# Attention and feed-forward on one core: GpSimd's additions made to wait for VectorE, another order of two half-array matmuls, and a new plan

## The chip, the core and the metric

The kernel runs on one core of a Trainium2 chip. The metric is the device time of one execution in microseconds, median of the runs. The core's engines each work through a queue of their own, in order: PE (TensorE, matmuls; its weight loads are shown as PEld), DVE (VectorE), ACT (ScalarE), POOL (GpSimd), and SP, which here only issues transfers.

## The reference, cut to what matters

```python
# q, k, v: (4, 8, 1152, 64)
q_pool = q.reshape(B, H, S // 2, 2, D).mean(axis=3)
scores = scale * np.matmul(q_pool, k.transpose(0, 1, 3, 2))
attn = np.exp(scores - np.max(scores, axis=-1, keepdims=True))
attn = attn / (np.sum(attn, axis=-1, keepdims=True) + 1e-09)
x = np.matmul(attn, v)          # then the heads side by side: (4 * 576, 8 * 64) = (2304, 512)
h = x @ w_in                     # 512 -> 2048
g = np.maximum(h, 0.0) + alpha * np.minimum(h, 0.0)
out = g @ w_out                  # 2048 -> 512
```

There are 32 heads with 576 pooled queries and 1152 keys each, and a feed-forward of 2304 tokens.

## The kernel before

Two heads are worked on together, as a pair, since a head has only 64 features: head 0 of the pair lies in rows 0 to 63 of the array of PE and head 1 in rows 64 to 127, and a matmul of 64 rows leaves the other half of the array to its neighbour. A pair's 576 queries are cut into two halves of 288, so there are 32 "half-heads", one after the other; in each of them nine blocks of 128 keys pass through four steps.

- **Scores** (line 951): eight matmuls a block, for x in four products, for i in the two heads. Numbers are split into a high and a low part so that float32 is kept: k1 and q1 are the high parts, k2 (line 699) and q2 (line 691) the low ones, and the fourth product subtracts the maxima. `ps` is a pair of PSUM banks, one for each head.
- **Exponentials** (line 968) on ACT, one for each head, from PSUM into the tile `pa`.
- **Sums of the exponentials** over the key blocks (line 981): of the seven additions of a half-head, the blocks 6 and 8 (`ADDS`) are added on DVE and five on POOL. At the end of a pair PE adds up the partitions (line 1017).
- **Weighted values** (line 995): 18 matmuls in a row at the end of the half-head, each of which the trace shows as two.

Between the score blocks stand the **maxima blocks** of the next pair: one matmul of 384 keys (line 818, one head each, heads taken in turn) or two of 288 (line 825, both on the same head), whose maximum DVE takes out of PSUM (line 839, into `bx`). 24 of the first kind and 8 matmuls of the second belong to a pair. The result of a pair is divided by its sums on DVE (line 1054, `r`), and split (line 1061 on ACT, line 1066 on DVE), and stored; all these DVE operations, like the low parts q2 and k2 and the conversion of the weights (lines 391 to 427), read two tensors from SBUF.

The feed-forward (line 479) runs partly between the last half-heads, and alone from about 445 us on, with 128-row matmuls.

The order of all instructions is made in Python before the kernel is built, by the class `Scheduler`. `add` records a task with an engine, a planned duration, what it reads and writes and a priority; `run` picks again and again the task that can start first by the planned times, with the smallest priority value among those within a slack, and `place` emits it. Tasks with `lock=True` (the DVE operations with two SBUF inputs and POOL's additions) are planned one after the other over both engines: `place` sets `lock_free` to the end of such a task and no other of them is planned before that. In the kernel before, that holds in the plan alone; on the chip each engine follows its own queue and waits only for its data. The numbers in the signature of `attention_ffn` are planned costs, slacks and priorities, and which PSUM banks scores, maxima and feed-forward may take early (`EARLY`) and after half-head 13 (`LATE`).

Of the kernel before, what the change touches and what calls it, by code (L numbers as in the profile page):

```python
# [108 lines left out]
class Scheduler:  # L109
# [3 lines left out]
    def __init__(self, col_cost, turn, to_pe, from_pe, slack, dma_fixed):  # L113
        self.tasks, self.ready = [], [[] for _ in range(5)]
        self.free = [0.0] * 5
        self.dma_free = 0.0
        self.now = 0.0
        self.col = 0
        self.lock_free = 0.0
        self.turn = turn  # L120
        self.col_cost, self.to_pe, self.from_pe, self.slack = col_cost, to_pe, from_pe, slack
        self.dma_fixed = dma_fixed
        self.hold = ()

    def add(self, eng, dur, emit, reads=(), writes=(), uses=(), deps=(), prio=0.0, col=0, size=0, kind=None, dma=False, lock=False, fixed=None):
        t = Task()
# [70 lines left out]
    def place(self, at, t):  # L197
        for b in t.takes:
            if b.t is None:
                b.ring.take(b)  # L200
        self.now = at
        t.emit()
        self.ready[t.eng].remove(t)
        dur = t.dur
        if t.eng == PE:
            if t.col != self.col:
                dur += ENTER if t.col else LEAVE
            self.col = t.col
        if t.lock:
            self.lock_free = at + dur  # L210
        self.free[t.eng] = at + dur
        t.end = at + dur
        if t.dma:
            self.dma_free = max(self.dma_free, t.end + 650) + t.size / DMA_RATE
            t.end = self.dma_free
            t.avail = t.end + (self.dma_fixed if t.fixed is None else t.fixed)
        else:
            t.avail = t.end + SYNC
        for n in t.next:
            n.left -= 1  # L220
            if not n.left:
                self.ready[n.eng].append(n)
# [3 lines left out]
def attention_ffn(  # L226
# [8 lines left out]
    NLO: int = 5,  # L235
    PB: int = 13,
    QB: int = 2,
    DF: int = 1985,
    D0: int = 1153.836,
    AQ: int = 0,  # L240
    F0: float = 7.572,
    F2: float = 0.839,
    FD: tuple = (1, 1, 1),
    WE: float = 24.0,
    WG: int = 1,
    WT: float = 6.74,
    WM: int = 2,
    WB: int = 300,
    WN: int = 2,
    TO_PE: int = 89,  # L250
    FROM_PE: int = 40,
    SLP: int = 45,
    SLA: int = 48,
    SLD: int = 138,
    QL: float = -0.025,
    KL: float = 1.207,
    KR: float = 1.497,
    KS: float = 0.082,
    M0: float = 1.211,
    E0: float = 1.868,  # L260
    BD: int = 7,
    SD: tuple = (3, 20),
    LD: tuple = (0, 33),
    TD: tuple = (3, 33),
    SR: float = 0.311,
    KQ: float = 0.342,
    KKB: int = 2,
    FQ: int = 1,
    FB: tuple = (1, 7),
    SF: int = -39,  # L270
    Q0: float = -2.2,
# [5 lines left out]
    ADDS: tuple = ((4, 6, 8), (6, 8)),  # L277
    PL: int = 0,
    LV: int = -2,
    LW: int = -8,  # L280
    GSB: int = 1,
    YSB: int = 4,
    R0: float = 4.187,
    R1: float = -5.36,
    R2: float = -7.727,
    R3: float = -0.231,
    W0: float = 5.34,
    W1: float = 1.69,
    W2: float = 18.088,
    W3: float = 0.137,  # L290
    YL: float = 0.337,
    MS: float = 0.136,
    EARLY: tuple = ((1, 2, 3, 4, 6), (0, 5, 6), ()),
    LATE: tuple = ((0, 1, 2, 3, 4, 5, 6), (0, 1, 2, 3, 4, 5, 6), (1, 2, 3, 4, 5, 6)),
    SWITCH: int = 13,
    GL: float = 23.364,
    COL: float = 0.151,
    HW: float = -1.194,
    XB: int = 4,
    PT: int = 17,  # L300
    VB: int = 4,
# [4 lines left out]
    QA: float = 1.0,  # L306
    REUSE: int = 6,
    NW: tuple = (464, 460, 460, 460, 460),
    RP: float = 31.088,
    RS: float = -1.017,  # L310
    RM: int = 30,
    RATE: float = 342.662,
):
    nc = tc.nc
# [33 lines left out]
    DMA_RATE = RATE  # L348
    sch = Scheduler(COL, SF, TO_PE, FROM_PE, (SLP, SLA, SLD, 0, 0), DF)
    add = sch.add  # L350

    def dt(name, shape, dtype):
        return dram.tile(shape, dtype, tag=name, name=name)
# [29 lines left out]
    def w_split(f, i, mag, prio, ring, left):  # L383
        w = Buf(ring)

        def high():
            w_tiles(f, i, w)
            nc.scalar.activation(out=wh[f, i], in_=mag.t, func=AF.Copy)

        def low():  # L390
            nc.vector.tensor_tensor(
                out=wl[f, i], in0=mag.t, in1=wh[f, i].bitcast(F32), op=ALU.subtract
            )

        t = add(ACT, act(DMO), high, reads=[mag], writes=[w], deps=left, prio=prio)
        add(DVE, dve(DMO), low, reads=[mag], writes=[w], deps=[t], prio=prio, lock=True)
        w_done[f, i] = w

    def w_convert(f, i, prio, release=(), ring=None, left=(), first=()):
# [6 lines left out]
            nc.scalar.activation(out=mag.t, in_=raw.t[:, :, 1].bitcast(F32), func=AF.Abs)  # L406

        def top():
            nc.vector.tensor_scalar(
                out=bits.t, in0=raw.t[:, :, 1], scalar1=3, scalar2=0x3FFFFFF8,  # L410
                op0=ALU.logical_shift_left, op1=ALU.bitwise_and,
            )

        def tail():
            nc.vector.scalar_tensor_tensor(  # L415
                out=bits.t, in0=raw.t[:, :, 0], scalar=29, in1=bits.t,
                op0=ALU.logical_shift_right, op1=ALU.bitwise_or,
            )

        def sign():  # L420
            nc.vector.scalar_tensor_tensor(
                out=bits.t, in0=raw.t[:, :, 1], scalar=-0x40000000, in1=bits.t,
                op0=ALU.bitwise_and, op1=ALU.bitwise_or,
            )

        def value():
            nc.vector.scalar_tensor_tensor(
                out=mag.t, in0=mag.t, scalar=F64_TINY, in1=bits.t.bitcast(F32),
                op0=ALU.is_ge, op1=ALU.mult,
            )  # L430
# [361 lines left out]
    def pair_max(n, w):  # L792
# [15 lines left out]
        for x, (t, j, i) in enumerate(items):  # L808
# [125 lines left out]
    def half_main(n, h, w):  # L934
# [7 lines left out]
        for c in range(NC):  # L942
# [1 line left out]
            p, ps = Buf(r_p), Buf(r_ps)  # L944
            at = n + h + c / NC

            def scores(ps=ps, s=s):
# [286 lines left out]
```

## Time and profile before

| | |
|---|---|
| time before, median of 3 runs | 842.04 us (840.05 to 842.55) |
| the profiled execution's own time | 839.95 us |
| its span | 838.2 us |
| busy PE / DVE / ACT / POOL | 825.2 / 567.0 / 437.4 / 262.4 us |

The span runs from the first to the last profiled instruction; 1.75 us of the execution's time lie around it. PE is nearly always busy in the sense that some matmul is in flight, but two matmuls of 64 rows can be in flight at once, so this share says nothing on how well the halves of the array are filled. The stages are the start (to about 20 us), attention with weight conversion (20 to 200), attention alone (200 to 390), attention mixed with the feed-forward (390 to 445), and the feed-forward.

### The profile page before, as it was taken

To read this page: it belongs to the slowest core of one execution; us is meant where nothing else is said; L and a number is where in the kernel's file an instruction comes from. 1 tells how busy PE (TensorE), PEld (TensorE's weight loads), DVE (VectorE), ACT (ScalarE), POOL (GpSimd) and SP (SyncE) were. 2 spreads that over 40 slices of the span, in tenths; PEclk is the share of its full clock that TensorE was granted. 3 is DMA by queue.
4 is the path that set the end of the run, shared out by engine and by line. 5 is a ranking of instruction groups with operands and counts; after the bars stand their busy time and mean duration, and the time that the engine had idled before them with its cause. 6 is when DMAs were issued, how large, how long until landed. Compare 5 with 4: busy or idle time off the path is not lost.

```text
span 838.2 us, 17447 instructions
## 1 busy us (share of the span) xinstructions
PE 825.2 (98%) x6690; PEld 691.4 (82%) x6690; DVE 567.0 (68%) x1035; ACT 437.4 (52%) x1124; POOL 262.4 (31%) x196
## 2 busy tenths in 40 slices
PE   8999999999999999999999999999999999999997
PEld 8767777676777777776779999998898988988986
DVE  7999999999998988889963799632242232322422
ACT  4657676675766676665754676643232233332321
POOL 5665665565565665654550000000000000000000
PEclk9999999999999999999999999999999999999999
DMA  8234345634354433323233768581330421300301
GB/s 274 58 89 164 82 144 140 197 115 123 87 179 122 122 116 77 83 72 109 69 124 121 248 195 260 177 228 58 91 92 3 120 59 46 91 0 1 91 1 45
DMA packets 67759, 93.71 MB, mean 112 GB/s; under 512 B 20004, under 2 KB 45404, under 8 KB 67676
## 3 DMA queue, kind: packets, MB, share of 16 engines
q1 hardware_dynamic: 65516, 88.18, 33.9%
q0 software_dynamic: 2160, 4.42, 3.6%
q8 instruction: 52, 0.85, 0.4%
q14 instruction: 31, 0.25, 0.1%
HBM read 73.48 MB, written 19.02 MB: 110 GB/s over the span
## 4 chain that ended last, share of the span: by engine, by line
PE 86%; DVE 9%; DMA 2%; issue 1%; ACT 1%; SPq 0%; DVEq 0%; ACTq 0%
PE bank L479 44%; PE bank L951 18%; PE bank L995 15%; PE bank L818 6%; DVE bx L839 3%; PE bank L1017 2%; DMA wraw<-wt 1%; DVE x L1066 1%; DVE pa L981 1%; PE bank L825 1%; PE bank L1129 1%; DMA kk<-kt 1%; DVE pos L515 1%; DVE r L1054 0%; DVE wbits L415 0%
## 5 line engine op out<-in xcount | busy, mean ns | idle before, releaser
L981 POOL TENSOR_TENSOR pa<-pa,pa 128x576 f32<-128x576 f32 x160 | 240.5, 1520 | 155.9 <-ACT pa L968 104.4
L839 DVE TENSOR_REDUCE bx<-bank 128x1 f32<-128x384 f32 (+1 forms) x448 | 214.0, 533 | 22.5 <-PE bank L818 19.9
L968 ACT ACTIVATE pa<-bank 128x288 f32<-128x288 f32 x576 | 199.7, 417 | 25.9 <-PE bank L951 17.4
L951 PE MATMUL bank<-q,k 64*128 64x288 f32 x1728 | 206.2, 311 | 0.8 <-DVE mq L923 0.6
L951 PEld LDWEIGHTS bank<-q,k 64*128 64x128 f32 x1728 | 163.3, 184 | 21.1 <-issue 9.3
L995 PE MATMUL bank<-pa,vv 128*64 128x288 f32 x1152 | 146.8, 409 | 0.0
L995 PEld LDWEIGHTS bank<-pa,vv 128*64 128x64 f32 x1152 | 79.9, 137 | 54.8 <-issue 3.8
L526 DVE TENSOR_TENSOR gw<-gs,gw 128x460 fp32r<-128x460 f32 (+1 forms) x55 | 35.1, 638 | 121.2 <-ACT gw L521 121.2
L951 PE MATMUL bank<-mq,neg 64*128 64x288 f32 x576 | 115.2, 291 | 0.0
L818 PE MATMUL bank<-k,q 64*128 64x384 f32 x384 | 110.1, 362 | 3.5 <-DVE bx L839 2.0
L521 ACT ACTIVATE gw<-gs 128x460 fp32r<-128x460 f32 (+1 forms) x55 | 32.4, 589 | 126.7 <-PE bank L479 115.2
L479 PE MATMUL bank<-wlow,wh 128*128 128x460 f32 (+1 forms) x320 | 93.0, 371 | 0.0
L479 PE MATMUL bank<-gw,wh 128*128 128x460 f32 (+1 forms) x320 | 92.8, 371 | 0.0
L951 PEld LDWEIGHTS bank<-mq,neg 64*128 64x128 f32 x576 | 83.3, 184 | 0.0
L818 PEld LDWEIGHTS bank<-k,q 64*128 64x128 f32 x384 | 62.4, 185 | 16.2 <-DVE bx L839 10.0
L515 DVE SCALAR_TENSOR_TENSOR gs<-gs,nal 128x460 f32<-128x460 f32 (+1 forms) x55 | 38.4, 699 | 52.9 <-ACT gs L510 52.9
L479 PE MATMUL bank<-x,wlow 128*128 128x288 f32 x480 | 66.3, 296 | 0.0
L479 PEld LDWEIGHTS bank<-wlow,wh 128*128 128x128 f32 x320 | 60.0, 188 | 7.1
L479 PE MATMUL bank<-gs,wlow 128*128 128x288 f32 x480 | 65.8, 295 | 0.1
L479 PEld LDWEIGHTS bank<-gw,wh 128*128 128x128 f32 x320 | 60.1, 188 | 6.8
L479 PEld LDWEIGHTS bank<-x,wlow 128*128 128x128 f32 x480 | 64.2, 188 | 1.6 <-issue 1.4
L479 PEld LDWEIGHTS bank<-gs,wlow 128*128 128x128 f32 x480 | 63.9, 188 | 1.4 <-DVE gs L526 0.5
(90 smaller groups left out, 1006.2 us busy)
## 6 DMA issues: line engine op xcount, KB each, us to landing
wraw<-wt SPq DMA_DIRECT2D x32, 512.0 KB
vv<-vt SPq DMA_DIRECT2D x32, 288.0 KB
xs<-x SPq DMA_DIRECT2D x32, 288.0 KB
x<-xs SPq DMA_DIRECT2D x32, 288.0 KB
kk<-kt SPq DMA_DIRECT2D x15, 576.0 KB
r<-rrd SPq DMA_DIRECT2D x64, 72.0 KB
yp<-ys SPq DMA_DIRECT2D x32, 144.0 KB
wlow<-xs SPq DMA_DIRECT2D x16, 288.0 KB
```

The costliest lines, as they stand in the source:

```text
L479: nc.tensor.matmul(out=ps[:, :n], lhsT=w[a, c // DMO][:, c % DMO:c % DMO + P], rhs=lo(hl), start=(first and i == 0), stop=(last and i == 2),)
L515: lambda: nc.vector.scalar_tensor_tensor(out=flat(pos), in0=flat(neg), scalar=nal[:, f:f + 1], in1=flat(pos), op0=ALU.mult, op1=ALU.add),
L521: ACT, act(n), lambda: nc.scalar.activation(out=gs.t[:, 0, :n], in_=flat(pos), func=AF.Copy),
L526: lambda: nc.vector.tensor_tensor(out=gs.t[:, 1, :n], in0=flat(pos), in1=gs.t[:, 0, :n].bitcast(F32), op=ALU.subtract),
L818: nc.tensor.matmul(out=ms.t[:, :JW], lhsT=w.q1.t[d, starts[t]:starts[t] + P], rhs=w.k1.t[d, j * JW:(j + 1) * JW], start=True, stop=True,)
L825: nc.tensor.matmul(out=ms.t[:, :S // 4], lhsT=w.rt.t[d, D - D * u:D - D * u + P], rhs=w.k1.t[d, c:c + S // 4], start=u == 0, stop=u == 1,)
L839: nc.vector.tensor_reduce(out=bx.t[:, at, j:j + 1], in_=ms.t[:, :m], axis=AX.X, op=ALU.max)
L951: nc.tensor.matmul(out=ps.t[i][:, :HQ], lhsT=k.t[d, s] if k else neg[d], rhs=r.t[d, q], start=x == 0, stop=x == len(pairs) - 1,)
L968: lambda ps=ps, p=p, i=i: nc.scalar.activation(out=p.t[:, i], in_=ps.t[i][:, :HQ], func=AF.Exp, scale=SCALE),
L981: lambda a=a, b=p, part=part, e=e: e.tensor_tensor(out=part.t, in0=a.t, in1=b.t, op=ALU.add),
L995: nc.tensor.matmul(out=av.t[i * D:(i + 1) * D, :HQ], lhsT=w.vv[i].t[:, e], rhs=p.t[:, i], start=(e == 0), stop=(e == NC - 1),)
L1017: nc.tensor.matmul(out=ps.t[g * 32:(g + 1) * 32, :HQ], lhsT=ones, rhs=acc[n + g // 2][j].t[:, g % 2], start=j == 0, stop=j == m - 1, tile_ ...
```

## The change

Three things change. First, `place` now keeps the last emitted DVE instruction with `lock=True` as `port`, and gives every emitted POOL instruction with `lock=True` a dependence on it, so that POOL waits on DVE's semaphore. (The conversions return their instruction now, so that it can be kept.) Second, a score block starts with the head whose half of the array the matmul planned before it did not use (`sch.tile`), and the exponentials follow that order. Third, the planned durations of maxima blocks are 108 and 165 instead of 130 and 190, and the numbers of the plan are set anew, so that the whole order is another one.

```diff
         self.hold = ()
+        self.port, self.after = None, None
+        self.tile = 1
...
         self.now = at
-        t.emit()
+        made = t.emit()
+        if t.lock and made is not None:
+            if t.eng == DVE:
+                self.port = made
+            elif self.port is not None:
+                self.after(made, self.port)
...
-    DF: int = 1985,
+    DF: int = 2010,
-    WT: float = 6.74,
+    WT: float = 5.439,
-    KR: float = 1.497,
+    KR: float = 2.229,
-    EARLY: tuple = ((1, 2, 3, 4, 6), (0, 5, 6), ()),
+    EARLY: tuple = ((1, 2, 3, 4, 5), (0, 5, 6), ()),
-    LATE: tuple = ((0, 1, 2, 3, 4, 5, 6), (0, 1, 2, 3, 4, 5, 6), (1, 2, 3, 4, 5, 6)),
+    LATE: tuple = ((0, 1, 2, 3, 4, 5, 6), (0, 5, 6), (3, 4, 5, 6)),
...
+    sch.after = lambda late, early: tc.add_manual_dep(
+        late.ins, early.ins.name, mybir.DependencyInfo(mybir.DependencyClass.Sync, mybir.DependencyReason.DATA),
+        reason="order on the shared port",
+    )
...
-            def rows(t=t, j=j, d=d, ms=ms):
+            def rows(t=t, j=j, d=d, ms=ms, i=i):
+                sch.tile = i
...
-            dur = 190 if rest else 130
+            dur = 165 if rest else 108
...
+            order = []
+
+            def scores(ps=ps, s=s, order=order):
                 pairs = ((w.k1, w.q1), (w.k1, w.q2), (w.k2, w.q1), (None, w.mq))
+                order.extend((1, 0) if sch.tile == 0 else (0, 1))
+                sch.tile = order[1]
                 for x, (k, r) in enumerate(pairs):
-                    for i, d in enumerate(both):
+                    for i in order:
+                        d = both[i]
...
-                    lambda ps=ps, p=p, i=i: nc.scalar.activation(
-                        out=p.t[:, i], in_=ps.t[i][:, :HQ], func=AF.Exp, scale=SCALE
+                    lambda ps=ps, p=p, o=order, i=i: nc.scalar.activation(
+                        out=p.t[:, o[i]], in_=ps.t[o[i]][:, :HQ], func=AF.Exp, scale=SCALE
                     ),
```

What the new order looks like in the instruction queues is shown at three places. All are in the stage of attention alone (DVE's and POOL's near 280 us of the trace before); line numbers of the changed kernel are 11 to 17 higher.

DVE's queue, at the end of a half-head, before: `r` and `x` are the results of the pair (lines 1054 and 1066), `q` and `k` the low parts of a later pair (lines 691 and 699), `bx` the maxima.

```order
L1054 TENSOR_TENSOR r<-avs,r 128x288 x2
L981 TENSOR_TENSOR pa_102<-pa_102,pa_91 128x576
L839 TENSOR_REDUCE bx_114<-bank_122 128x1
L839 TENSOR_REDUCE bx_114<-bank_119 128x1
L839 TENSOR_REDUCE bx_114<-bank_121 128x1
L1066 TENSOR_TENSOR x_4110<-r,x_4110 128x288
L1066 TENSOR_TENSOR x_4114<-r,x_4114 128x288
L981 TENSOR_TENSOR pa_102<-pa_102,pa_93 128x576
L691 TENSOR_TENSOR q_4125<-qs,q_3710 128x576
L699 TENSOR_TENSOR k_4135<-kk,k_3756 128x1152
```

The same place in the changed kernel (lines 1071, 1083, 702, 710):

```order
L1071 TENSOR_TENSOR r<-avs,r 128x288
L998 TENSOR_TENSOR pa_101<-pa_101,pa_91 128x576
L1071 TENSOR_TENSOR r<-avs,r 128x288
L1083 TENSOR_TENSOR x_4115<-r,x_4115 128x288
L851 TENSOR_REDUCE bx_114<-bank_118 128x1
L851 TENSOR_REDUCE bx_114<-bank_124 128x1
L851 TENSOR_REDUCE bx_114<-bank_123 128x1
L1083 TENSOR_TENSOR x_4141<-r,x_4141 128x288
L998 TENSOR_TENSOR pa_101<-pa_101,pa_93 128x576
L702 TENSOR_TENSOR q_4155<-qs,q_3761 128x576
L710 TENSOR_TENSOR k_4157<-kk,k_3837 128x1152
```

The two results are no longer side by side: one DVE addition now stands between the two `r`, and one split goes ahead of the three maxima instead of both behind them. The additions and the low parts follow as before.

POOL's queue at the same place, before: `pa` are the exponentials and their sums, `qs` the second half of a later pair's queries, which POOL loads.

```order
L981 TENSOR_TENSOR pa_102<-pa_89,pa_90 128x576 [waits Activation_49]
L981 TENSOR_TENSOR pa_102<-pa_102,pa_92 128x576 [waits DVE_49,Activation_49]
L981 TENSOR_TENSOR pa_103<-pa_94,pa_97 128x576 [waits Activation_49]
L981 TENSOR_TENSOR pa_103<-pa_103,pa_100 128x576 [waits Activation_49,Pool_49]
L981 TENSOR_TENSOR pa_103<-pa_103,pa_88 128x576 [waits Activation_49,Pool_49]
L981 TENSOR_TENSOR pa_96<-pa_89,pa_90 128x576 [waits Activation_49]
L656 DMA qs<-qt 128x576 [waits DMAHW4_49,DMASW2_49,DVE_49]
L981 TENSOR_TENSOR pa_96<-pa_96,pa_92 128x576 [waits DVE_49,Activation_49]
```

In the changed kernel:

```order
L998 TENSOR_TENSOR pa_101<-pa_89,pa_90 128x576 [waits Activation_49]
L998 TENSOR_TENSOR pa_101<-pa_101,pa_92 128x576 [waits DVE_49]
L998 TENSOR_TENSOR pa_103<-pa_94,pa_97 128x576 [waits DVE_49,Activation_49]
L998 TENSOR_TENSOR pa_103<-pa_103,pa_99 128x576 [waits Activation_49,Pool_49]
L667 DMA qs<-qt 128x576 [waits DMAHW2_49,DMASW2_49]
L998 TENSOR_TENSOR pa_103<-pa_103,pa_88 128x576 [waits Activation_49,Pool_49]
L998 TENSOR_TENSOR pa_96<-pa_89,pa_90 128x576 [waits Activation_49]
L998 TENSOR_TENSOR pa_95<-pa_98,pa_100 128x576 [waits DVE_49,PE_49,Activation_49]
```

The third row, the first addition of a new half-head, now waits for DVE too, by its position in the plan for the low part `k` that ends the DVE rows above; the load of `qs` moves up by two additions. Of the 160 additions of line 981, 33 wait for DVE before the change and 71 after it.

PE's queue at a single maxima block of head 0 between two score blocks, before: the first two rows end a score block (head 0, head 1), and the bank with the lower number is always that of head 0.

```order
L951 MATMUL bank_119<-mq_111,neg 128x288
L951 MATMUL bank_122<-mq_111,neg 128x288
L818 MATMUL bank_120<-k_3359,q_3340 128x384
L951 MATMUL bank_123<-q_2602,k_2645 128x288
L951 MATMUL bank_124<-q_2602,k_2645 128x288
L951 MATMUL bank_123<-q_3040,k_2645 128x288
L951 MATMUL bank_124<-q_3040,k_2645 128x288
```

In the changed kernel, again with a single maxima block of head 0 (line 830) between two score blocks (line 968):

```order
L968 MATMUL bank_121<-mq_112,neg 128x288
L968 MATMUL bank_122<-mq_112,neg 128x288
L830 MATMUL bank_123<-k_3392,q_3345 128x384
L968 MATMUL bank_120<-q_2978,k_3025 128x288
L968 MATMUL bank_119<-q_2978,k_3025 128x288
L968 MATMUL bank_120<-q_3587,k_3025 128x288
L968 MATMUL bank_119<-q_3587,k_3025 128x288
```

After the maxima block of head 0 the score block now starts with the higher bank, that of head 1. Counted over the whole queue, neighbours on the same half among the score and maxima matmuls fall by 210, from 297 to 87 with the fillers and the two-matmul maxima blocks counted; changes between matmul shapes (64 rows, 128 rows, 64 or 32 columns) rise from 98 to 103, and the filler matmuls of the start (line 1129) from 136 to 150. The feed-forward's matmuls are as many as before.

## Rows read from the trace of the kernel before

**Rows 1.** The page's line of busy time, share and instructions.
```profile
PE 825.2 (98%) x6690; PEld 691.4 (82%) x6690; DVE 567.0 (68%) x1035; ACT 437.4 (52%) x1124; POOL 262.4 (31%) x196
```

**Rows 2.** Stages: length, busy PE, PEld, DVE, ACT, POOL (instructions), clock, DMA share, GB/s.
```profile
20.00:200.00 180.00, 177.60 (x1844) 133.86 (x1844) 173.65 (x337) 120.25 (x337) 113.27 (x77) 1.00 0.44 125
200.00:390.00 190.00, 187.67 (x1979) 140.57 (x1978) 169.52 (x320) 123.15 (x345) 112.74 (x81) 1.00 0.36 106
390.00:445.00 55.00, 55.00 (x525) 42.86 (x524) 43.70 (x59) 34.06 (x97) 25.48 (x16) 1.00 0.33 104
```

**Rows 3.** Shares by engine of the chain that ended last.
```profile
PE 86%; DVE 9%; DMA 2%; issue 1%; ACT 1%; SPq 0%; DVEq 0%; ACTq 0%
```

**Rows 4.** Waits, whole span: who waited for whom, us in total, times, longest.
```profile
POOL pa L981 <- ACT pa L968: 104.4, 38, 6.1
...
ACT rt L680 <- DMA qs<-qt: 15.7, 6, 3.9
...
PEld bank L818 <- DVE bx L839: 10.0, 36, 1.0
PEld bank L951 <- issue: 9.3, 22, 0.5
```

**Rows 5.** Lines 1066 and 981: duration ns min/median/max, first and last start.
```profile
L1066 DVE TENSOR_TENSOR x<-r,x x32: 443/656/1673, 72.1 to 461.5; 128x288 fp32r<-128x288 f32 x32
L981 POOL TENSOR_TENSOR pa<-pa,pa x160: 1389/1427/4784, 21.4 to 434.4; 128x576 f32<-128x576 f32 x160
...
L981 DVE TENSOR_TENSOR pa<-pa,pa x64: 684/748/1975, 29.6 to 440.1; 128x576 f32<-128x576 f32 x64
```

**Rows 6.** Timeline of DVE and POOL, 278 to 289 us: start, length, instruction.
```profile
280.14 2.24 DVE L1066 TENSOR_TENSOR x<-r,x 128x288 fp32r<-128x288 f32 x2
...
283.64 1.34 DVE L699 TENSOR_TENSOR k<-kk,k 128x1152 fp32r<-128x1152 f32 x1
...
279.07 2.99 POOL L981 TENSOR_TENSOR pa<-pa,pa 128x576 f32<-128x576 f32 x2 [1.87 <-ACT k L684]
285.41 4.32 POOL L981 TENSOR_TENSOR pa<-pa,pa 128x576 f32<-128x576 f32 x3 [3.35 <-ACT pa L968]
```

**Rows 7.** Timeline of DVE: the first and the last overtaken operations of the stages.
```profile
51.18 1.56 DVE L981 TENSOR_TENSOR pa<-pa,pa 128x576 f32<-128x576 f32 x1
...
174.94 1.67 DVE L1066 TENSOR_TENSOR x<-r,x 128x288 fp32r<-128x288 f32 x1
...
202.47 2.24 DVE L1066 TENSOR_TENSOR x<-r,x 128x288 fp32r<-128x288 f32 x2
...
382.20 1.96 DVE L981 TENSOR_TENSOR pa<-pa,pa 128x576 f32<-128x576 f32 x1
...
434.76 1.66 DVE L1054 TENSOR_TENSOR r<-avs,r 128x288 f32<-128x288 f32 x1
```

**Rows 8.** Line 818 on PE by stage, first 20 to 200, then 200 to 390.
```profile
L818 PEld LDWEIGHTS bank<-k,q 64*128 64x128 f32 x185 | 29.7, 184 | 10.3 <-DVE bx L839 6.8 <-ACT rs L1029 1.4 <-issue 0.5
...
L818 PEld LDWEIGHTS bank<-k,q 64*128 64x128 f32 x177 | 28.8, 184 | 4.4 <-DVE bx L839 2.9 <-issue 0.9
```

**Rows 9.** Timeline of PE: pairs of maxima blocks between scores, 287 and 360 us.
```profile
287.54 0.72 PE L951 MATMUL bank<-q,k 64*128 64x288 f32 x6
...
288.30 0.76 PE L951 MATMUL bank<-q,k 64*128 64x288 f32 x6
...
360.43 0.36 PE L951 MATMUL bank<-q,k 64*128 64x288 f32 x1
...
361.37 0.62 PE L951 MATMUL bank<-q,k 64*128 64x288 f32 x5
```

**Rows 10.** Timeline of ACT and PE about 340 us: a load of queries awaited.
```profile
344.46 0.26 ACT L680 ACTIVATE rt<-qs 128x64 fp32r<-128x64 f32 x1 [3.94 <-DMA qs<-qt]
...
339.88 4.59 PE L995 MATMUL bank<-pa,vv 128*64 128x288 f32 x36
```

**Rows 11.** Timeline of PE at the start: filler matmuls.
```profile
1.06 4.42 PE L1129 MATMUL bank<-even 64*128 64x256 f32 x38 [1.06 <-DVE ones L1114]
```

More of the change, by code (lines that the diff above doesn't have):

```diff
@@ L237, in attention_ffn @@
     QB: int = 2,
-    DF: int = 1985,
+    DF: int = 2010,
     D0: int = 1153.836,
     AQ: int = 0,
-    F0: float = 7.572,
+    F0: float = 7.519,
     F2: float = 0.839,
     FD: tuple = (1, 1, 1),
-    WE: float = 24.0,
+    WE: float = 24.18,
     WG: int = 1,
-    WT: float = 6.74,
+    WT: float = 5.439,
     WM: int = 2,
@@ L249, in attention_ffn @@
     WN: int = 2,
-    TO_PE: int = 89,
+    TO_PE: int = 88,
     FROM_PE: int = 40,
-    SLP: int = 45,
-    SLA: int = 48,
+    SLP: int = 39,
+    SLA: int = 78,
     SLD: int = 138,
     QL: float = -0.025,
-    KL: float = 1.207,
-    KR: float = 1.497,
-    KS: float = 0.082,
-    M0: float = 1.211,
+    KL: float = 1.242,
+    KR: float = 2.229,
+    KS: float = 0.067,
+    M0: float = 1.209,
     E0: float = 1.868,
@@ L262, in attention_ffn @@
     SD: tuple = (3, 20),
-    LD: tuple = (0, 33),
+    LD: tuple = (1, 33),
     TD: tuple = (3, 33),
-    SR: float = 0.311,
+    SR: float = 0.906,
     KQ: float = 0.342,
@@ L269, in attention_ffn @@
     FB: tuple = (1, 7),
-    SF: int = -39,
-    Q0: float = -2.2,
+    SF: int = -33,
+    Q0: float = -2.408,
     Q1: float = 2.605,
@@ L276, in attention_ffn @@
     AB: int = 10,
-    ADDS: tuple = ((4, 6, 8), (6, 8)),
+    ADDS: tuple = ((2, 4, 6, 8), (6, 8)),
     PL: int = 0,
     LV: int = -2,
-    LW: int = -8,
+    LW: int = -5,
     GSB: int = 1,
@@ L283, in attention_ffn @@
     R0: float = 4.187,
-    R1: float = -5.36,
-    R2: float = -7.727,
+    R1: float = -5.889,
+    R2: float = -4.86,
     R3: float = -0.231,
@@ L288, in attention_ffn @@
     W1: float = 1.69,
-    W2: float = 18.088,
+    W2: float = 16.818,
     W3: float = 0.137,
-    YL: float = 0.337,
-    MS: float = 0.136,
-    EARLY: tuple = ((1, 2, 3, 4, 6), (0, 5, 6), ()),
-    LATE: tuple = ((0, 1, 2, 3, 4, 5, 6), (0, 1, 2, 3, 4, 5, 6), (1, 2, 3, 4, 5, 6)),
+    YL: float = 0.326,
+    MS: float = 0.134,
+    EARLY: tuple = ((1, 2, 3, 4, 5), (0, 5, 6), ()),
+    LATE: tuple = ((0, 1, 2, 3, 4, 5, 6), (0, 5, 6), (3, 4, 5, 6)),
     SWITCH: int = 13,
@@ L297, in attention_ffn @@
     COL: float = 0.151,
-    HW: float = -1.194,
+    HW: float = -0.27,
     XB: int = 4,
@@ L308, in attention_ffn @@
     NW: tuple = (464, 460, 460, 460, 460),
-    RP: float = 31.088,
-    RS: float = -1.017,
+    RP: float = 31.836,
+    RS: float = -2.623,
     RM: int = 30,
@@ L390, in low @@
         def low():
-            nc.vector.tensor_tensor(
+            return nc.vector.tensor_tensor(
                 out=wl[f, i], in0=mag.t, in1=wh[f, i].bitcast(F32), op=ALU.subtract
@@ L408, in top @@
         def top():
-            nc.vector.tensor_scalar(
+            return nc.vector.tensor_scalar(
                 out=bits.t, in0=raw.t[:, :, 1], scalar1=3, scalar2=0x3FFFFFF8,
@@ L414, in tail @@
         def tail():
-            nc.vector.scalar_tensor_tensor(
+            return nc.vector.scalar_tensor_tensor(
                 out=bits.t, in0=raw.t[:, :, 0], scalar=29, in1=bits.t,
@@ L420, in sign @@
         def sign():
-            nc.vector.scalar_tensor_tensor(
+            return nc.vector.scalar_tensor_tensor(
                 out=bits.t, in0=raw.t[:, :, 1], scalar=-0x40000000, in1=bits.t,
@@ L426, in value @@
         def value():
-            nc.vector.scalar_tensor_tensor(
+            return nc.vector.scalar_tensor_tensor(
                 out=mag.t, in0=mag.t, scalar=F64_TINY, in1=bits.t.bitcast(F32),
@@ L945, in half_main @@
             at = n + h + c / NC
-            def scores(ps=ps, s=s):
+            order = []
+            def scores(ps=ps, s=s, order=order):
                 pairs = ((w.k1, w.q1), (w.k1, w.q2), (w.k2, w.q1), (None, w.mq))
+                order.extend((1, 0) if sch.tile == 0 else (0, 1))
+                sch.tile = order[1]
                 for x, (k, r) in enumerate(pairs):
-                    for i, d in enumerate(both):
+                    for i in order:
+                        d = both[i]
                         nc.tensor.matmul(
```

## The prediction

> **What bounds the kernel now.** I read the busy shares first, then the stages, then the chain that ended last, the waits, and last the timeline around DVE's longest operations. PE has a matmul in flight for 98% of the span [rows 1], in every stage [rows 2], and 86% of the chain runs over it [rows 3]. That share flatters it in attention, where one matmul of 64 rows leaves half of the array to another. The number beside it decides: from 20 to 200 us, where the first weights are converted too, DVE is busy 173.65 of 180 us, 96%; from 200 to 390 it is 169.52 of 190, 89%; from 390 to 445 it is 43.70 of 55 while PE is busy throughout [rows 2]. So the first of these stages hangs on DVE about as much as on PE, the second less, and in the third PE has feed-forward matmuls to fill every wait. Behind 445 us nothing of the change is at work: the feed-forward has the same matmuls.
>
> Part of DVE's busy time is no work. The split of line 1066 takes 0.443 us at best and 1.673 at worst, an addition of line 981 on DVE 0.684 at best and 1.975 at worst, and what is added is about the length of one POOL addition, 1.427 us at the median [rows 5]. The timeline shows how: POOL adds from 279.07 on, twice in a row, and the two splits of 280.14, worth 0.9 us, take 2.24 [rows 6]. The second POOL addition belongs behind the low part k of 283.64 in the order in which the planner emitted the two engines' instructions; it ran 4.5 us early, as its exponentials were ready, and DVE stood still for it.
>
> **The edge from DVE to POOL.** I went through all DVE operations with two SBUF inputs that ran over their usual length while a POOL addition was on. The excess is 40 us in all. In 25 of them the addition had been emitted behind the DVE operation, and started ahead of it: 7 between 20 and 200 us, 8.2 us together, 10 between 200 and 390, 12.1 us, and 8 behind 390, 9.2 us; the first and the last of the first two stages, and the last of all, are in [rows 7]. The new dependence forbids just these 25. The remaining 11 us are of additions that were planned ahead of the DVE operation and ran late; they stay possible.
>
> The page "SBUF — State Buffer" of the Trainium skill, section "Who interferes with whom", says that a VectorE instruction with two SBUF inputs and a GpSimd one that reads SBUF exclude each other for the whole instruction, and whichever starts first wins. The trace agrees, 0.443 against 1.673 us in line 1066. By that rule the stall isn't removed but handed to POOL, whose additions would be late by the same 29.5 us; if POOL had no room, the sum below would be 0 for this term.
>
> POOL has room: it is busy 112.74 of 190 us [rows 2], and waits 104.4 us in all for exponentials [rows 4]. Queued behind an addition that waits are the other additions of the half-head and POOL's loads of queries; for the sums wait PE's matmuls of line 1017, for the loads ACT.
>
> What do 8.2 us of DVE's time give in the first stage? At least nothing, if PE's own order sets the pace, at most 8.2. With DVE at 96% I take 5. In the second stage the bounds are 0 and 12.1. There PE waits for DVE's maxima only 2.9 us [rows 8], and DVE has 20 us idle; I take 2. Behind 390 us I take 0 of 9.2, because PE is busy all 55 us with matmuls that have to be done.
>
> **The idle half first.** 210 neighbours on the same half disappear. If each held up the other half by one spacing, it would be dear; but look at two stretches from one score block's start to the next, with two maxima blocks in between: where the queue has two such neighbours, at 287.54, the next block starts 0.76 us later, and where it has none, at 360.43, 0.94 us later [rows 9]. So the waits for a free bank and for DVE outweigh it. Lower bound 0; upper bound: 85 single maxima blocks at 0.18 us (0.76 less an estimated 0.58 for four pairs of score matmuls at 0.12 and half a maxima matmul), 15 us. I take 1.5, near the row with the longer time and no neighbours.
>
> **What the new plan costs.** PE changes its shape 5 times more. The sequencer's gaps ahead of score blocks are 9.3 us in 22 [rows 4], 0.42 each, so 0 to 2.1 us; I take 1. (The page "TensorEngine Tiling (Array Packing)" of the Trainium skill, "Key Properties", says that a change of tiling mode drains the engine, which speaks against this change; by the gap above it is 2.1 us.) 14 more fillers at 4.42/38 = 0.116 us [rows 11] are 1.6 us at most; they stand where PE waits for the first keys, so 0.3. In the late bank plan maxima have three banks instead of seven, as they already have before half-head 13; there PE's loads waited 6.8 us for DVE, later 2.9 [rows 8], so up to 3.9 us are lost; I take 0.7, since DVE is less loaded late. The shorter planned maxima and the other numbers only order the queues.
>
> **Sum.** -5 - 2 - 1.5 + 1 + 0.3 + 0.7 = -6.5 us. The profiled execution took 839.95 us (span 838.2, 1.75 around it) and would take 833.5; the median of the runs is 2.1 above it, so the forecast is 842.0 - 6.5 = **835.5 us**.
>
> **Rivals.**
> - *All of the stall comes back.* If DVE sets the pace in the second stage as well, the first gives 8.2, the second half of 12.1, the halves 3, less 2 of costs: -15.2, 826.8 us. For it speaks DVE's share, 89% and more; against it the small waits of PE for DVE.
> - *Nothing comes back.* The stall lies under the 36 passes of line 995, 4.59 us long [rows 10], in which DVE has little that PE needs at once; or POOL's other additions, planned ahead but late, stall DVE in its place, so that the edge doesn't do what it is for. Then only the 1.5 and the 2 remain: 842.5 us. For it speaks the second stage, where DVE is free of the stall at 282.4 and PE doesn't wait; against it the first stage.
> - *POOL is late with the queries.* The edge holds back POOL's queue, and with it the loads of queries. ACT already waits 15.7 us for them, in 6 places [rows 4]; at 344.46 its wait of 3.94 us ends just when the weighted block of 339.88 ends [rows 10], so that there any later landing delays the exponentials, and PE behind them. 15 pairs have such a load, two of them at the start; I count 13. From 6.5/13 = 0.5 us a pair it eats the gain; the addition of 280.5 may move by up to 4.5 us, to the end of k, and the load stands two additions, 2.9 us, earlier in the new queue, which leaves 1.6 us. At 1 us a pair the time is 835.5 + 13 = 848.5 us. Against it speaks that 9 of the 15 loads land before ACT asks for them.
>
> **How the numbers follow.** The forecast (829 to 839.5 by its own bounds) has a chance of 0.55, the whole stall 0.14, nothing 0.18, slower 0.13. For 8 times in 10 the range goes from 827, the larger gain, to 843.5, no gain with the costs at their upper ends; it leaves out most of the slower case. About 0.3%, 2.5 us, is what a measurement here can tell from no change: faster is below 839.5, slower above 844.6. The forecast and the larger gain are faster (0.69, and a little of the third), no change 0.18, slower 0.12.
>
> **What would show it.** In the profile of the changed kernel line 1066 should have a median near 0.45 us and DVE's busy time should fall by 20 us or more, most of it before 390 us; POOL's additions should wait on DVE lines. The half-heads of the first stage, from one weighted block to the next, should shorten more than those of the second. ACT's wait for `qs` should stay near 15 us; if it doubles, the slower case has come. If DVE's busy time falls and the stages keep their lengths, the second rival holds. If the pairs from 200 us on shorten by more than 0.5 us each, I have priced the halves, or the stall there, too low.

## The result and the profile after

The changed kernel takes **834.26 us** (median of 6 runs, 833.61 to 834.63) against 841.28 of the kernel before in the same comparison (839.66 to 842.8). The ratio is 0.9917, with a 95% interval of 0.9904 to 0.9929: 7.0 us faster, by more than the bound of 0.3%. The forecast was 835.5, 6.5 us under the median of before. The total is right; what follows shows that the three terms behind it are not.

Busy time, span and chain of the page of the changed kernel, beside [rows 1, 3]:

```profile
span 832.6 us, 17390 instructions
...
PE 822.6 (99%) x6704; PEld 685.9 (82%) x6704; DVE 545.5 (66%) x1035; ACT 437.0 (52%) x1124; POOL 254.7 (31%) x196
...
PE 96%; DVE 2%; issue 0%; ACT 0%; POOL 0%; DVEq 0%; ACTq 0%
```

DVE is busy 21.5 us less with the same 1035 instructions, and has left the chain (9% to 2%). The stages, with the columns of [rows 2]:

```profile
20.00:200.00 180.00, 178.07 (x1855) 131.38 (x1854) 166.32 (x338) 121.98 (x339) 106.24 (x78) 1.00 0.43 123
200.00:390.00 190.00, 189.79 (x2004) 141.37 (x2001) 164.38 (x325) 124.22 (x352) 113.02 (x81) 1.00 0.38 109
390.00:445.00 55.00, 55.00 (x522) 43.58 (x521) 35.89 (x57) 33.74 (x95) 24.39 (x16) 1.00 0.32 105
```

DVE gives up 7.33, 5.14 and 7.81 us. That comes from single operations getting shorter, as the durations (minimum, median, maximum in ns) of the split, now line 1083, and of the additions, now line 998, show beside [rows 5]:

```profile
L1083 DVE TENSOR_TENSOR x<-r,x x32: 445/450/1161, 73.0 to 455.8; 128x288 fp32r<-128x288 f32 x32
...
L998 POOL TENSOR_TENSOR pa<-pa,pa x160: 1401/1425/3856, 21.1 to 433.1; 128x576 f32<-128x576 f32 x160
...
L998 DVE TENSOR_TENSOR pa<-pa,pa x64: 685/749/1951, 30.4 to 435.0; 128x576 f32<-128x576 f32 x64
```

The median of the split falls from 656 to 450 ns. The excess of DVE's operations over their usual length, counted as for the prediction, was 40 us and is 13 us now, in 28 operations, none of them overtaken. (Line 409, now 420, one of the conversions, is not in this count: it reads one tensor and not two, but beside an addition it took up to 1323 ns before and 1424 after, at a median of 419 in both.) The place of [rows 6] in the timeline of the changed kernel (start, length, instruction, wait):

```profile
275.70 0.45 DVE L1083 TENSOR_TENSOR x<-r,x 128x288 fp32r<-128x288 f32 x1
...
276.23 1.41 POOL L998 TENSOR_TENSOR pa<-pa,pa 128x576 f32<-128x576 f32 x1 [2.32 <-DVE x L1083]
...
279.22 1.35 DVE L710 TENSOR_TENSOR k<-kk,k 128x1152 fp32r<-128x1152 f32 x1
...
280.71 1.42 POOL L998 TENSOR_TENSOR pa<-pa,pa 128x576 f32<-128x576 f32 x1 [3.07 <-DVE k L710]
```

POOL now waits for the split and for k, as the edge asks. Waits of the whole span, beside [rows 4] (total, times, longest):

```profile
POOL pa L998 <- ACT pa L985: 43.6, 31, 5.4
ACT pa L985 <- PE bank L968: 27.5, 96, 0.6
POOL pa L998 <- DVE x L1083: 27.4, 11, 3.0
...
PEld bank L830 <- DVE bx L851: 8.8, 39, 0.5
...
ACT rt L691 <- DMA qs<-qt: 8.5, 4, 3.5
...
PEld bank L968 <- ACT pa L985: 7.9, 34, 0.4
...
PEld bank L968 <- issue: 6.8, 16, 0.5
PEld bank L830 <- issue: 6.3, 14, 0.5
```

POOL's wait for exponentials falls from 104.4 to 43.6 us and turns into waits for DVE. The queries are waited for less, 8.5 instead of 15.7. One wait has grown: PE's loads for the scores wait 7.9 us for exponentials; before it was 1.8 us in 6 places. PE's sequencer ("issue") holds up the scores less than before, 6.8 instead of 9.3 us, and the maxima more, 6.3 instead of 1.8.

The starts of the weighted blocks (line 995, now 1012) in the timelines tell where the time came from (us from the span's start, one block for each half-head, counted from 0; the end is that of the span). "Edge", "halves" and "banks" are versions that are told of below.

| block | before | after | plan of before, edge | the same, edge and halves | the same, with banks | after with banks |
|---|---|---|---|---|---|---|
| 13 | 200.9 | 197.9 | 198.2 | 199.6 | 195.9 | 194.9 |
| 25 | 352.6 | 350.2 | 346.5 | 351.6 | 343.8 | 344.2 |
| 28 | 395.3 | 392.2 | 387.9 | 393.7 | 384.8 | 385.4 |
| 31 | 432.6 | 427.4 | 424.8 | 430.6 | 421.8 | 420.9 |
| end | 838.2 | 832.6 | 829.4 | 836.0 | 826.9 | 825.2 |

After the change 3.0 us are gained by block 13; between 13 and 25 0.6 are lost again, but in that stretch the changed kernel also does a feed-forward step of 1.85 us, which the kernel before does later; 0.7 are gained from there to block 28 and 2.5 behind it.

### The profile page after: what moved, and what is told of

Read it like the earlier page. It is cut to its first block, busy times and chain, and to the rows that moved or that the text cites. A ratio compares the mean times of both kernels' runs of the same rounds, so it can differ in the third digit from the quotient of the medians.

```text
span 832.6 us, 17390 instructions
## 1 busy us (share of the span) xinstructions
PE 822.6 (99%) x6704; PEld 685.9 (82%) x6704; DVE 545.5 (66%) x1035; ACT 437.0 (52%) x1124; POOL 254.7 (31%) x196
## 4 chain that ended last, share of the span: by engine, by line
PE 96%; DVE 2%; issue 0%; ACT 0%; POOL 0%; DVEq 0%; ACTq 0%
PE bank L490 49%; PE bank L968 19%; PE bank L1012 17%; PE bank L830 7%; PE bank L1034 2%; DVE bx L851 2%; PE bank L837 1%; PE bank L1146 1%; POOL pa L998 0%; DVE pa L998 0%; PE bank L867 0%; ACT pa L985 0%; DVE q L702 0%; PE bank L918 0%; ACT mq L929 0%
## 5 line engine op out<-in xcount | busy, mean ns | idle before, releaser
L998 POOL TENSOR_TENSOR pa<-pa,pa 128x576 f32<-128x576 f32 x160 | 234.3, 1500 | 171.3 <-ACT pa L985 43.6
L968 PE MATMUL bank<-q,k 64*128 64x288 f32 x1728 | 194.5, 308 | 0.8 <-DVE mq L935 0.5
L968 PEld LDWEIGHTS bank<-q,k 64*128 64x128 f32 x1728 | 145.9, 184 | 20.3 <-ACT pa L985 7.9
L968 PE MATMUL bank<-mq,neg 64*128 64x288 f32 x576 | 103.2, 291 | 0.0
L968 PEld LDWEIGHTS bank<-mq,neg 64*128 64x128 f32 x576 | 71.8, 184 | 0.0
L998 DVE TENSOR_TENSOR pa<-pa,pa 128x576 f32<-128x576 f32 x64 | 51.5, 804 | 21.1 <-POOL pa L998 21.1
```

What stands on the lines that cost most here:

```text
L968: nc.tensor.matmul(out=ps.t[i][:, :HQ], lhsT=k.t[d, s] if k else neg[d], rhs=r.t[d, q], start=x == 0, stop=x == len(pairs) - 1,)
L998: lambda a=a, b=p, part=part, e=e: e.tensor_tensor(out=part.t, in0=a.t, in1=b.t, op=ALU.add),
```

## Experiments

Two theories stood at first: T1, the edge carries the gain; T2, the halves and the plan carry it. "us" are medians of the runs. Since the kernels ran beside runs of before with medians from 840.2 to 841.3, differences between them are worked out from the ratios, times 840.5 us.

**The changed kernel without the edge**, and **with the halves in fixed order**:

```diff
-                self.after(made, self.port)
+                pass
```

> The changed kernel without the dependence of POOL's additions on DVE; queues, halves and plan stay as in the changed kernel. If the edge carries the gain (first theory), POOL's additions overtake DVE again, line 1083 goes back to a worst time near 1.67 us, DVE's busy time rises by 15 us or more and the time by 4 to 7 us, to 838 to 841. If halves and plan carry it (second theory), the time stays within 1.5 us of 834.3 though DVE is stalled again.

```diff
-                order.extend((1, 0) if sch.tile == 0 else (0, 1))
+                order.extend((0, 1))
```

> The changed kernel with every score block started at head 0 again; edge and plan stay. First theory: the halves are worth 1.5 us, so 835 to 837. Second theory: they are worth 4 us or more, 838 or above, and most of it lies where PE sets the pace, between 200 and 390 us.

Without the edge: 845.97 us, ratio 1.006 (1.0038 to 1.0083), slower than before by 5.0; the edge is worth 12.0 us in the new plan, well beyond T1's range. The split's row there shows the long operations back at 1675 ns:

```profile
L1083 DVE TENSOR_TENSOR x<-r,x x32: 445/459/1675, 74.3 to 468.8; 128x288 fp32r<-128x288 f32 x32
```

With fixed halves: 832.74 us, ratio 0.9903 (0.9886 to 0.992). Both theories missed: without the alternation the kernel is not slower, but 1.2 us faster, within the intervals. PE's loads for scores waited 0.4 us for exponentials, not 7.9.

**The plan of before with the edge alone**, and **with the halves alone**: the kernel before with only the edge of the diff, or only the edits in `rows` and `scores`.

> The kernel before with the dependence alone: old plan, old halves. First theory: the 29.5 us of overtaken DVE operations go, and 5 to 8 us of time with them, 833 to 836 against 841.3. Second theory: DVE's busy time falls by 25 us or more and the time by less than 1.5 us, since PE did not need DVE earlier.

> The kernel before with the idle half first alone: old plan, no dependence. First theory: 1.5 us faster, 839 to 841 against 841.3. Second theory: 4 us faster or more, 837.5 or below.

The edge alone: 831.2 us, ratio 0.9888 (0.9869 to 0.9908), 9.4 us faster, 1.8 us under T1's range, and faster than the whole change; T2 falls. The halves alone: 848.65 us, ratio 1.0097 (1.0077 to 1.0116), **8.2 us slower**, which neither theory allowed. The row that answers is the one that had grown in the changed kernel:

```profile
PEld bank L968 <- ACT pa L985: 15.6, 56, 1.0
```

Theory A came from it. In the kernel before, a score block starts with the lower bank of its pair, and the exponentials free the lower bank first too. If blocks alternate, while the banks stay tied to the heads, a block can start with the bank that the block before it on that pair freed second. ACT's queue in the changed kernel, at the half-head that begins at 230 us, shows it (bank read by each exponential):

```order
L985 ACTIVATE pa_88<-bank_121 128x288
L985 ACTIVATE pa_88<-bank_120 128x288
L985 ACTIVATE pa_89<-bank_119 128x288
L985 ACTIVATE pa_89<-bank_122 128x288
L985 ACTIVATE pa_90<-bank_120 128x288
L985 ACTIVATE pa_90<-bank_121 128x288
```

The third block (`pa_90`) starts with bank 120, which the first freed second. The timeline of PE's loads and ACT there:

```profile
230.67 1.41 ACT L985 ACTIVATE pa<-bank 128x288 f32<-128x288 f32 x4 [0.29 <-PE bank L968]
...
231.53 0.43 PEld L968 LDWEIGHTS bank<-q,k 64*128 64x128 f32 x6 [0.39 <-ACT pa L985]
...
232.42 1.42 ACT L985 ACTIVATE pa<-bank 128x288 f32<-128x288 f32 x4 [0.34 <-PE bank L968]
...
233.18 0.43 PEld L968 LDWEIGHTS bank<-q,k 64*128 64x128 f32 x6 [0.26 <-ACT pa L985]
...
234.07 1.37 ACT L985 ACTIVATE pa<-bank 128x288 f32<-128x288 f32 x4 [0.23 <-PE bank L968]
...
234.84 0.43 PEld L968 LDWEIGHTS bank<-q,k 64*128 64x128 f32 x6 [0.25 <-ACT pa L985]
```

PE waits for ACT, starts one exponential late, and then ACT waits for PE: every second block both stand still for about 0.3 us, and four blocks take 234.84 - 231.53 = 3.31 us.

**The plan of before with edge and halves; with the matmuls alternating and the exponentials in fixed order; with the exponentials alternating and the matmuls in fixed order** (the last two without the edge):

```diff
+                o = (1, 0) if sch.tile == 0 else (0, 1)
+                sch.tile = o[1]
-                order.extend((1, 0) if sch.tile == 0 else (0, 1))
-                sch.tile = order[1]
+                order.extend((0, 1))
...
-                    for i in order:
+                    for i in o:
```

This is the edit for the matmuls alone, beside the changed kernel's lines; for the exponentials alone it is `order.extend(o)` and `for i in (0, 1)`.

> The plan of before with both other parts of the change, the edge and the alternating halves; beside the version with the edge alone (831.2 us) it prices the halves under the edge, and beside the changed kernel (834.3 us) the new plan. Theory A (alternating halves cost a wait of PE's weight loads on the exponentials, because a block that starts with head 1 needs first the bank that the block before it freed last; the edge hides part of it, since ACT and PE are then less late): 832 to 834.5 us, PE's loads of scores wait 6 to 12 us for exponentials, and the new plan is worth 0 to -2. Rival B (the halves hurt only through GpSimd's overtaking, which the edge forbids): within 0.8 us of 831.2, and the waits for exponentials stay near 2.3 us; then the new plan costs 3.

> The plan of before, no edge; the matmuls of a score block start with the idle half, but the exponentials are taken in fixed order, head 0 first. Theory A: the bank that is needed first is then always freed second where a block starts with head 1, and the exponential of head 0 waits for the matmuls that end last: at least as slow as both together (848.6 us), 848 to 855, and PE's loads wait 15 us or more for exponentials. Rival B (the changed order of ACT is what hurts, the order of the matmuls gains as forecast): 837 to 841 us, waits for exponentials near the 1.8 us of before.

> The plan of before, no edge; the matmuls of a score block in fixed order, head 0 first, but the exponentials alternate as in the changed kernel. Theory A: where the exponential of head 1 goes first, the bank of head 0, which the next users need first, is freed second: 843 to 850 us, PE's loads wait 8 us or more for exponentials. Rival B: as slow as both together, 847 to 850, since ACT's order is the cause; a rival C, that the place of the matmuls alone costs (changes of halves within the array): 840 to 842, as before.

Edge and halves: 837.89 us, ratio 0.9973 (0.9962 to 0.9985), 7.1 slower than the edge alone. So the halves hurt with the edge too, and rival B falls. A is right that the waits come, but it put both too low: 6 to 12 us of waits, where 15.7 were measured, and 832 to 834.5 us. The matmuls alone: 844.2, ratio 1.0047 (1.003 to 1.0063). The exponentials alone: 848.33, ratio 1.0094 (1.008 to 1.0108). The queues give the number of score blocks whose first bank was freed by the second exponential of an earlier block, and the profiles the waits:

| version | such blocks of 288 | PE's score loads wait for exponentials, us (times) | against its fixed order, us |
|---|---|---|---|
| before; with edge | 1; 1 | 1.8 (6); 2.3 (7) | |
| halves; with edge | 166; 166 | 15.6 (56); 15.7 (59) | +8.2; +7.1 |
| matmuls alone | 110 | 9.3 (36) | +4.0 |
| exponentials alone | 99 | 6.4 (24) | +7.9 |
| after; with fixed halves | 142; 5 | 7.9 (34); 0.4 (2) | +1.2 |

Matmuls alone landed between A and B, with 9.3 us of waits where A wanted 15 or more: 110 blocks start on the late bank, and not all. Exponentials alone fits A in time and not in its waits, 6.4 us for 8 or more; it fits its rival B in time as well, and rival C falls. It pays as much as both together with 99 late blocks. That the exponential of the head whose matmuls end last sometimes goes first doesn't explain it: that is so in 112 blocks of either version, and ACT waits 23.4 us for score matmuls in both. Matmuls alone also has the idle half first, and exponentials alone has not, so that what this order gains may be part of the difference; that was not tested.

**The edge in both directions** on the plan of before, so that DVE too waits for the addition planned ahead of it (A and B in its expectation are theories on this question alone):

```diff
             if t.eng == DVE:
+                if self.pool is not None:
+                    self.after(made, self.pool)
                 self.port = made
-            elif self.port is not None:
-                self.after(made, self.port)
+            else:
+                if self.port is not None:
+                    self.after(made, self.port)
+                self.pool = made
```

> The plan of before with the edge, and the same edge the other way too: DVE's operations with two SBUF inputs wait for the GpSimd addition planned ahead of them. Nothing can then run beside an addition that would stall it, and the 11 to 13 us by which late additions still lengthen DVE's operations become waits. Theory A (DVE stands still for the same addition either way, and its queue in order behind it too; waiting for an addition that has not even started is worse): slower than the one-way edge, 833 to 840 us, DVE's busy time falls by 10 us or more and its waits for additions rise by more. Rival B (a stalled operation costs more than one that starts late, since the port's turn is lost): 828 to 831 us.

832.9 us, ratio 0.9909 (0.9895 to 0.9923): 1.8 us above the one-way edge, and the intervals overlap; it lies just under the range of A and above that of B, so time decides for neither. No operation is stretched any longer (the split is line 1087 here), and what was stall is now waiting, as the durations and the two largest waits on DVE's side show:

```profile
L1087 DVE TENSOR_TENSOR x<-r,x x32: 449/451/459, 71.9 to 453.6; 128x288 fp32r<-128x288 f32 x32
```
```profile
DVE pa L1002 <- POOL pa L1002: 13.4, 8, 4.3
DVE wmag L442 <- POOL pa L1002: 4.8, 4, 1.6
```

DVE is busy 530.1 us, 13.7 less than with the one-way edge, and its waits for POOL's additions rise by more, from 15.5 to 41.1 us, as A has it. There is no gain: the remaining stall is not worth a wait.

**The edge for the first 70 additions** (to about 200 us) and **for the first 140** (to about 380 us), on the plan of before:

```diff
-            elif self.port is not None:
-                self.after(made, self.port)
+            else:
+                if self.port is not None and self.adds < 70:
+                    self.after(made, self.port)
+                self.adds += 1
```

> The plan of before with the edge for the first 70 of GpSimd's 160 additions alone, that is up to about 200 us. Theory P (the prediction: the edge gives most in the first stage, -5 of -7, since DVE is nearest to its limit there): 834.5 to 836. Theory S (from the starts of the weighted blocks in the runs so far: with the edge they come 2.7 us earlier at 200 us, 7.4 earlier at 395): the first stage gives only 2 to 3.5 of the 9 us: 836.5 to 838.5.

> The plan of before with the edge for the first 140 of the 160 additions, that is up to about 380 us. Theory P: the second stage adds 2 to the first and what lies behind is worth 0, so the time is that of the whole edge, 831.2, within 0.8. Theory S: the second stage gives 4 to 5.5, and what lies behind gives 1 to 2 more, so that this run is at 832 to 833.5.

837.01 us, ratio 0.9956 (0.9943 to 0.9969), and 833.16, ratio 0.991 (0.9897 to 0.9922). By the ratios the first stage gives 3.7 us, the second 3.9 and the last 20 additions 1.8 (this last one with overlapping intervals). Both times lie in the ranges of theory S; P falls for the first two stages, and its 0 for the last is not excluded.

The profiled executions agree. They give the time for the same work, from the start of one weighted block to that of another (us, plan of before):

| edge | start to block 13 | block 13 to 28 | block 28 to the end |
|---|---|---|---|
| none (before) | 200.9 | 194.4 | 442.9 |
| first 70 additions | 196.8 | 194.4 | 442.3 |
| first 140 | 197.9 | 190.9 | 442.7 |
| all | 198.2 | 189.7 | 441.5 |

A count of work in a fixed stretch of time would mislead here. From 390 to 445 us the whole edge has more feed-forward matmuls than before, but fewer score matmuls, since it is further on (before, then the whole edge; two lines of each):

```profile
L951 PE MATMUL bank<-q,k 64*128 64x288 f32 x168 | 16.7, 306 | 0.0
L479 PE MATMUL bank<-x,wlow 128*128 128x288 f32 x63 | 9.9, 304 | 0.0
```
```profile
L968 PE MATMUL bank<-q,k 64*128 64x288 f32 x144 | 14.0, 304 | 0.0
L490 PE MATMUL bank<-x,wlow 128*128 128x288 f32 x96 | 13.8, 299 | 0.0
```

**Alternating halves with the banks exchanged**, on the plan of before with the edge, and on the changed kernel: whichever head starts writes the pair's lower bank.

```diff
-                    for i in order:
+                    for b, i in enumerate(order):
                         d = both[i]
...
-                            out=ps.t[i][:, :HQ], lhsT=k.t[d, s] if k else neg[d], rhs=r.t[d, q],
+                            out=ps.t[b][:, :HQ], lhsT=k.t[d, s] if k else neg[d], rhs=r.t[d, q],
...
-                        out=p.t[:, o[i]], in_=ps.t[o[i]][:, :HQ], func=AF.Exp, scale=SCALE
+                        out=p.t[:, o[i]], in_=ps.t[i][:, :HQ], func=AF.Exp, scale=SCALE
```

> The plan of before with the edge and the alternating halves, but the matmuls of the half that starts write the first of the block's two banks, whichever head that is, so that the bank needed first is again the one that was freed first (261 of 288 blocks, as in the fixed order; 96 where halves alternate with banks tied to heads). Theory A (the halves cost 6.7 us by the banks' release alone): 829 to 832 us, at or under the 831.2 of the fixed order, PE's loads of scores wait under 4 us for exponentials. Rival D (the idle half first costs by itself, on the array, and the waits are its consequence): 836 to 839, as with both, waits near 15 us.

> The changed kernel with the same exchange of banks. Theory A: the halves' cost of 1.5 us goes: 830.5 to 833 us, at or under the 832.7 of the changed kernel with fixed halves, and the 7.9 us of waits for exponentials fall under 2. If the idle half first gives what the prediction took for it, -1.5, the time is 831. Rival D: 834 to 835.5, as the changed kernel.

829.34 us, ratio 0.987 (0.9856 to 0.9885), and **827.2 us**, ratio 0.984 (0.9828 to 0.9853), the fastest version of all: 13.4 us under the kernel before and 6.5 under the change. Rival D falls. Theory A holds in the first; in the second its waits come out, but the time is 3.3 us under its range. The waits of the changed kernel with exchanged banks, and the same half-head in its timeline:

```profile
PEld bank L968 <- ACT pa L985: 0.4, 2, 0.2
```
```profile
227.09 1.40 ACT L985 ACTIVATE pa<-bank 128x288 f32<-128x288 f32 x4 [0.31 <-PE bank L968]
...
227.93 0.42 PEld L968 LDWEIGHTS bank<-q,k 64*128 64x128 f32 x5 [0.19 <-ACT pa L985]
...
228.70 2.89 ACT L985 ACTIVATE pa<-bank 128x288 f32<-128x288 f32 x8 [0.21 <-PE bank L968]
```

Of the three waits of PE one is left, and ACT runs eight exponentials in a row in 2.89 us; in the changed kernel two groups of four, with the wait between them, take from 232.42 to 235.44, 3.02 us. The exponentials still alternate between the heads here, so it is the bank and not ACT's order of heads that costs. Tied to the heads, the banks cost 8.7 us in the old plan and 6.5 in the new one, by the versions with and without the exchange. Beside the fixed order of the same plan, the idle half first gains 1.5 us in the old plan (the intervals overlap) and 5.3 in the new one (they don't). Why it gives more in the new plan was not separated.

## Why the prediction was right in the total, and where it was not

The total is right by luck: errors of opposite sign cancel. A path of versions from before to after, by ratios: the edge -9.4, the halves +7.1, the new plan -4.7; together -7.0. The other order of the last two: edge -9.4, plan with fixed halves +1.3, halves +1.2. The prediction had -7, -1.5 and +2.

**The edge: the mechanism right, the size too small.** The 25 overtaken operations are gone, the median of the split is 450 ns as forecast, DVE's busy time fell by 21.5 us, 12.5 of it ahead of 390 us, and POOL had room. But the edge gives 9.4 us in the old plan and 12.0 in the new one. The step that was mis-sized is the share of the stall that comes back by stage: -5, -2 and 0 of 8.2, 12.1 and 9.2 us were taken, and 3.7, 3.9 and 1.8 were measured, the last one not clear of noise. The first was too much. The second was too little, because the prediction looked only at PE's waits for the maxima. In that stretch PE waits longer for the additions of DVE and POOL, before it sums over the partitions (line 1017, now 1034). PE's waits from 200 to 390 us, before and with the edge alone:

```profile
PEld bank L1017 <- DVE pa L981: 5.6, 8, 1.6
...
PEld bank L818 <- DVE bx L839: 2.9, 10, 1.0
PEld bank L1017 <- POOL pa L981: 2.2, 5, 0.4
...
PE bank L1017 <- DVE pa L981: 1.6, 2, 1.1
PEld bank L1017 <- issue: 1.3, 3, 0.4
```
```profile
PEld bank L1034 <- issue: 3.5, 8, 0.4
...
PEld bank L830 <- DVE bx L851: 1.4, 7, 0.3
```

With the edge the sums wait for neither DVE nor POOL, only 2.2 us longer for the sequencer, and the waits for maxima halve. The runs with part of the edge fit: with the first 70 additions the loads of the sums still wait 5.6 us for DVE and 2.2 for POOL in that stretch, with the first 140 only 1.6 for DVE. That PE is busy was no reason for a 0 in the third stage: from 200 to 390 us it is busy 187.67 of 190 us [rows 2], and the same work still shortens. But no load of PE waits for DVE or POOL from 390 to 445 us in either version, so whether that stage gives anything stays open. The sentence of the Trainium skill, page "SBUF — State Buffer", section "Who interferes with whom", that the one that starts first keeps the other out, agrees with the trace: a split took 445 ns or up to 1161 in the changed kernel, and 459 at most once both engines kept to the plan. That the stall is handed to POOL is what the waits show (27.4 us for the split alone), and POOL's lateness cost nothing that can be seen.

**The idle half first: the wrong sign.** -1.5 was taken, with bounds of 0 and -15; a loss was not priced at all. As changed it costs 1.2 us (not resolved) in the new plan, 7.1 to 8.2 in the old one. The step that failed is that the change of order was priced by the array alone. The exponentials "follow that order", as the change says, within a block, but the bank of the next block was not thought of. The neighbours on the same half were indeed worth something, 5.3 us in the new plan once the banks follow, and 1.5 in the old one (not resolved): 8.7 of cost less 1.5 make the 7.1, and 6.5 less 5.3 the 1.2.

**The new plan: not a cost.** +2.0 was taken. With fixed halves it is +1.3, within what the intervals allow; with the alternating halves of the change it is -4.7, with exchanged banks -2.5. Part of this is visible: the new plan has 142 blocks on a late bank in place of 166, and 7.9 us of waits in place of 15.7. Which of its numbers does it was not tried. The term for shape changes, +1 with 2.1 as its upper end, was too small if all of the sequencer's waits belong to it: with the edge, PE's loads, all lines together, wait 23.6 us for the sequencer in the old plan and 26.1 in the new one with fixed halves, 2.5 more. The late maxima banks were taken at 0.7; from 200 to 390 us the loads of maxima wait 2.7 us for DVE in the changed kernel and 1.4 with the edge alone (above), so 1.3 more:

```profile
L830 PEld LDWEIGHTS bank<-k,q 64*128 64x128 f32 x176 | 28.1, 184 | 8.1 <-issue 4.5 <-DVE bx L851 2.7 <-ACT pa L985 0.5
```

**The rivals.** Nothing comes back: refuted by the edge's own 9.4 us. Late queries: ACT's waits for them nearly halved [rows 4]. All of the stall comes back: it put the edge at about 14 us; the 9.4 of the old plan are nearer to the 7 that were taken, the 12.0 of the new one nearer to the rival, and the halves' loss hid it. The last sentence of the prediction, that pairs from 200 us on would shorten if the stall there were priced too low, answers for the edge alone (block 25 is 6.1 us earlier, block 13 only 2.7), and is hidden in the whole change.

The luck in numbers: on the path above the edge gave 2.4 us more than forecast and the new plan 6.7 more, while the halves took 8.6 more; with the last two in the other order it is 2.4, 0.7 and 2.7.

## What to carry to other kernels

An exclusion between two engines that only the plan knows must be enforced across their queues; where the later engine has slack, the wait costs nothing, but making both wait in turn gains nothing either. Whoever changes the order in which buffers are filled must follow each buffer to its next user: swap the buffers with the order, or the one needed first is the one freed last. A busy share of 99% on matmuls that use half of the array says nothing on room; compare the time for the same work, from one instruction to another, and not the work in a fixed stretch of time. Whoever prices a stall looks at every wait for the stalled engine in that stretch, not at the first one found.

## What was not expected of the hardware

A wait of 0.2 to 0.4 us of PE's weight loads, which the busy shares don't show, makes PE and ACT wait for each other in turn, and 56 to 59 such waits of 15.6 us in all went with 7 to 8 us of time. Turning 13.7 us of stretched DVE operations into waits, once the overtaken ones were gone, changed the time by nothing that could be resolved. An operation with one input in SBUF (line 409) is stretched beside POOL's additions too: 1323 ns against at most 429 in the version with the edge both ways.
